# A two-layer decode step on one core: the fold's masks and sums on GpSimd, one row's LayerNorm on ScalarE and GpSimd, PV between the scores

## The chip, the cores and the metric

The kernel runs on one core of a Trainium2 chip. The metric is the device time of one execution in microseconds (us). The version before takes 1202.7 us, the median of three runs (1202.06 to 1204.01).

## The reference

Eight rows `x` (one token each, 512 numbers, bfloat16) go twice through the same two blocks, with the same weights and caches both times:

```
x = x + A(layernorm(x))     # attention: 32 query heads, 8 key/value heads,
                            # 8192 cached positions of 128 numbers, wq 512x4096, wo 4096x512
x = x + B(layernorm(x))     # silu(h @ w1) @ w2, w1 512x1792, w2 1792x512
```

A query head group of four shares one key/value head: scores are q.k / sqrt(128), softmax over the 8192 positions, then the sum of the values, then wo. Each row has its own cache of 8 x 8192 x 128 keys and as many values, in bfloat16: 128 MiB of keys and 128 MiB of values in all. In the second pass the caches are needed again.

## The kernel before, in words

**Tasks and positions.** A task is one (layer, row b, key/value head g): 2 x 8 x 8 = 128 tasks. Its keys and its values are 2 MiB each, loaded in four granules of 512 KB into slots of an arena (`NSLOT = 27` slots). A task has `GPT = 8` positions, two for each granule (`GPG = 2`). One Python loop over the position `p` writes all instructions in order; each engine then executes its own instructions in that order, with semaphores between engines.

**The order of the tasks.** Of a row's 32 key granules (8 heads of 4) the last `KEEP = 20`, heads 3 to 7, stay in the arena from layer 0 to layer 1. So a row's heads 3 to 7 in layer 0 ("kept" tasks) come shortly before the same heads in layer 1, which load values alone. Between them stand five or six tasks of heads 0 to 2 (of layer 0 of a later row, or of layer 1 of an earlier one), which load keys and values, four and four. Meanwhile the row's "chain" runs: output projection, residual, LayerNorm, MLP, LayerNorm and query projection of this one row, spread over the positions. `plan_loads` gives each load the position where it is needed and the one after which its slot is free; SyncE issues them in the order of need, and waits for the slot.

**One task, by lines of before.** VectorE transposes each key granule in place (L466), `LT` positions ahead of the position; TensorE makes the scores of the granule at the odd positions (L543). After the task, in the next eight positions (the table `soft`): `softmax_max` at 0 (VectorE L554, L556, then GpSimd's all-reduce over partitions `tops`, L559), `softmax_shift` and `softmax_exp` at 2 (VectorE L563, L566, ScalarE L570), `softmax_sum` at 4 (VectorE makes `ssm`, L577, GpSimd's all-reduce `ssa`, L580), `emit_pt` at 5 (TensorE transposes P, L589, ScalarE copies to PT, L593), `softmax_rcp` at 7 (L600). The values are multiplied `LP` positions after the scores (`emit_pv`, L608), at odd positions too, behind the scores.

**The fold.** The result of PV lies in a PSUM bank `OTp` as 128 partitions x 512: of each row only one of four blocks of 128 columns is its own. `emit_own` and `emit_fold` (`FOLD_AT` positions later) bring them together into 128 x 4. In most tasks ScalarE copies the bank to `E` (L624) and TensorE multiplies four blocks with masks `sel` (L640). In the tasks of layer 1 whose keys are kept (`eased`), VectorE masks and sums the four blocks (L629, L632) and TensorE does one multiplication with `hm` (L645). `emit_norm`, `FOLD` positions after the last PV's place, divides by the softmax sum (L655). `add_heads` multiplies four finished heads of a row with wo (L739).

**The chain.** `chain_of` is a list of stages. In each position as many are taken as are needed to end `EARLY = 4` positions ahead of the row's first task of layer 1. `ln_stages` has three: a sum and its all-reduce (L663, L665), centring, squares and their sum and all-reduce (L671 to L680), the reciprocal root by `NEWTON = 3` steps on VectorE (L685 to L699). `settle` adds `SETTLE` empty stages behind them; `project` cuts a projection into pieces (L721).

The initial all-reduces and the LayerNorm of all eight rows, at the start and at the end, go through the same functions with n = 8.

Of the kernel before, what the change touches and what calls it, by code (L numbers as in the profile page):

```python
# [5 lines left out]
HQ = 32  # L6
DH = 128
SM_SCALE = DH ** -0.5
LN_EPS = 1e-5
RSQRT_SEED = float(0x5F3759DF)  # L10
NEWTON = 3

GRP = 8
GPT = 8
GPG = 2
NSLOT = 27
KEEP = 20
LT = 2
PRE = 10
LP = 14  # L20
EARLY = 4
WO_FROM = 36
NTP = 2
# [7 lines left out]
PAIR = 2  # L31
REACH = 32767
PAIR_ALL = False
FOLD = 3
FOLD_AT = 2
ACT_FOLD = True
NQS = 4
CW = 32
SETTLE = 2

BF16 = mybir.dt.bfloat16
FP32 = mybir.dt.float32
# [181 lines left out]
def _build(ctx, nc, A_x, A_k_cache, A_v_cache, A_wq, A_wo, B_w1, B_w2, out):  # L224
# [68 lines left out]
    tr = sb([128, B], FP32, "tr")  # L293
    s1 = sb([128, B], FP32, "s1")
    s1a = sb([128, B], FP32, "s1a")
    xc = sb([128, KT, B], FP32, "xc")
    sq = sb([128, KT, B], FP32, "sq")
    xnT = sb([128, KT, B], BF16, "xnT")
# [88 lines left out]
    with nc.Block() as block:  # L387

        @block.sync
        def _(sync_eng):  # L390
# [183 lines left out]

            def softmax_sum(ti):
                st = ti % NST
                op(dve, lambda: dve.tensor_scalar(  # L577
                    ssm[st][:, :], hm[:, :], rs[st][:, 0:1], None, op0=ALU.mult),
                   reads=["hm", f"rs{st}"], writes=[f"ssm{st}"])
                op(pool, lambda: pool.partition_all_reduce(ssa[st][:, :], ssm[st][:, :], 128, bass.bass_isa.ReduceOp.add),  # L580
                   reads=[f"ssm{st}"], writes=[f"ssa{st}"])
# [32 lines left out]
                ]  # L614
                mm_group(steps, reads=[r_half(slot, 0), r_half(slot, 1), f"PT{pb}"], writes=[f"OT{ob}"])

            def eased(ti):
                layer, _b, g = tasks[ti]
                return layer == 1 and (g, 0) in kept

            def emit_own(ti):
                ob = ti % 2
                if not eased(ti) and ACT_FOLD:
                    op(act, lambda: act.copy(E[:, :], OTp[ob][:, :]), reads=[f"OT{ob}"], writes=["E"])  # L624
                    return
                for x in range(CPB):
                    ot = OTp[ob][:, x * DH:(x + 1) * DH]
                    if x == 0:
                        op(dve, lambda: dve.tensor_scalar(E[:, 0:DH], ot, own_x[:, 0:1], None, op0=ALU.mult),  # L629
                           reads=[f"OT{ob}", "own_x"], writes=["E"])  # L630
                    else:
                        op(dve, lambda x=x, ot=ot: dve.scalar_tensor_tensor(  # L632
                            E[:, 0:DH], ot, own_x[:, x:x + 1], E[:, 0:DH], op0=ALU.mult, op1=ALU.add),
                           reads=[f"OT{ob}", "own_x", "E"], writes=["E"])

            def emit_fold(ti):
                ob = ti % 2
                if not eased(ti) and ACT_FOLD:
                    steps = [
                        lambda x=x: pe.matmul(OTp[ob][:, 0:REP], E[:, x * DH:(x + 1) * DH], sel[:, x, :],  # L640
                                              start=(x == 0), stop=(x == CPB - 1))
                        for x in range(CPB)
                    ]
                else:
                    steps = [lambda: pe.matmul(OTp[ob][:, 0:REP], E[:, 0:DH], hm[:, :], start=True, stop=True)]  # L645
                mm_group(steps, reads=["E", "hm", "sel"], writes=[f"OT{ob}"])
# [11 lines left out]
            def ln_stages(xv, rx, n):  # L658

                xcv, sqv, xnv = xc[:, :, 0:n], sq[:, :, 0:n], xnT[:, :, 0:n]  # L660

                def first():
                    op(dve, lambda: dve.tensor_reduce(s1[:, 0:n], xv.rearrange("p k b -> p b k"), AX.X, ALU.add),  # L663
# [18 lines left out]
                def third():  # L682
                    v, y, t = vr[:, 0:n], yr[:, 0:n], tr[:, 0:n]
                    vi, yi = v.bitcast(INT32), y.bitcast(INT32)
                    op(dve, lambda: dve.tensor_scalar(v, s1a[:, 0:n], 1.0 / D, LN_EPS, op0=ALU.mult, op1=ALU.add),  # L685
                       reads=["s1a"], writes=["vr"])
                    op(dve, lambda: dve.tensor_scalar(yi, vi, 1, None, op0=ALU.logical_shift_right),
                       reads=["vr"], writes=["yr"])
                    op(dve, lambda: dve.tensor_scalar(yi, yi, -1.0, RSQRT_SEED, op0=ALU.mult, op1=ALU.add),
                       reads=["yr"], writes=["yr"])  # L690
                    if n == 1:
                        scale = 1.0
                        for _n in range(NEWTON):
                            op(dve, lambda: dve.tensor_scalar(t, y, y, v, op0=ALU.mult, op1=ALU.mult),  # L694
                               reads=["yr", "vr"], writes=["tr"])
                            op(dve, lambda: dve.tensor_scalar(y, t, -3.0 * scale ** 2, y, op0=ALU.add, op1=ALU.mult),  # L696
                               reads=["tr", "yr"], writes=["yr"])
                            scale *= -2.0 * scale ** 2
                        op(dve, lambda: dve.tensor_scalar(xnv, xcv, y, 1.0 / scale, op0=ALU.mult, op1=ALU.mult),  # L699
                           reads=["xc", "yr"], writes=["xnT"])  # L700
                        return
# [60 lines left out]
            def block_stages(xs, rxs, n, fine=False):  # L762

                x0, x1, x2 = xs
                r0, r1, r2 = rxs
                parts = 2 if fine else 1
# [12 lines left out]
                def attended():  # L779
                    add_residual(x1, r1, x0, r0, n, CW if n == 1 else n)  # L780

                st = [attended] + ln_stages(x1, r1, n) + settle
                st += joined(project(w1_sb, "w1", FT, KT, lambda k: xnT[:, k, 0:n], "xnT", n, parts), expo)
                st += [silu, idle]
                st += joined(
                    project(w2_sb, "w2", KT, FT, lambda k: hsT[:, k * n:(k + 1) * n], "hsT", n, parts),
                    lambda: add_residual(x2, r2, x1, r1, n, n))
                return st

            def joined(pieces, then):  # L790
                last = pieces[-1]
# [7 lines left out]
            def query(n, dst_of, rdst, parts=1):  # L799
                return joined(  # L800
                    project(wq_sb, "wq", HQ, KT, lambda k: xnT[:, k, 0:n], "xnT", n, parts),
                    lambda: op(
                        dve,
                        lambda: dve.tensor_copy(dst_of, MISC[:, 0:HQ * n].rearrange("p (h b) -> p h b", b=n)),
                        reads=["MISC"], writes=rdst,
                    ))

            def chain_of(b):
                xs = [XT[n][:, :, b:b + 1] for n in range(3)]
                st = block_stages(xs, ["XT0", "XT1", "XT2"], 1, True)  # L810
                st += ln_stages(xs[2], "XT2", 1) + settle
                return st + query(1, QT2[b % 2][:, 0:HQ].rearrange("p (h b) -> p h b", b=1), [f"QT2_{b % 2}"], 4)

            summed = [0] * (B + 1)
            heads = [[] for _ in range(B + 1)]
# [38 lines left out]
            first1 = {b: min(task_at[(1, b, g)] for g in range(HKV)) * GPT for b in range(B)}  # L854
            ntask = len(tasks)

            for p in range(NG + LP + GPT + FOLD + 1):
                tq = (p + LQ) // GPT
                if (p + LQ) % GPT == 0 and tq < ntask:
# [5 lines left out]
                emit_t_until(p + LT)  # L865
                if p % GPG == GPG - 1 and p < NG:
                    emit_s(p)
                if p % GPG == GPG - 1 and 0 <= p - LP < NG:
                    emit_pv(p - LP)
                copied = p - LP - GPT  # L870
                if copied >= 0 and copied % GPT == 0 and copied // GPT < ntask:
# [8 lines left out]
                if chain:  # L880
                    left = max(1, first1[chain_b[0]] - EARLY - p)
                    for _n in range(-(-len(chain) // left)):
                        chain.pop(0)()
                elif p >= WO_FROM and heads[turn[0]] and not (p < NG and tasks[p // GPT][0] and (tasks[p // GPT][2], 0) in kept
                                             and turn[0] < B):
                    add_heads(turn[0])
                done = p - LP - GPT - FOLD
                if done >= 0 and done % GPT == 0 and done // GPT < ntask:
# [61 lines left out]
```

## Time and profile before

| | |
|---|---|
| median of three runs | 1202.7 us (1202.06 to 1204.01) |
| the profiled execution | 1203.2 us, of which the span is 1201.2 us |
| TensorE busy | 811.5 us (68%), weight loads 505.4 us |
| VectorE busy | 735.7 us (61%) |
| ScalarE busy | 274.0 us (23%) |
| GpSimd busy | 117.9 us (10%), 300 instructions |
| DMA, loads | 465.12 MB, mean 389 GB/s, 99.2% of 16 engines' span |

Times are microseconds from the start of the span. The page's digits are the busy share of forty equal slices in tenths. In a timeline or a group, PE is TensorE, DVE VectorE, ACT ScalarE, POOL GpSimd, SP SyncE; a row of the timeline has the start, the duration, engine, line, operation and tiles, and in brackets the idle time of the engine before it and what ended that ("issue": nothing that the profile shows). In a row of windows the columns are the stretch, its length, the busy time of TensorE, its weight loads, VectorE, ScalarE and GpSimd with the number of instructions, the granted TensorE clock, DMA's share and GB/s. Reloads, waits and semaphores are not counted as busy.

### The profile page before, as it was taken

Reading aid. Unit: us, or ns where it says so; the run is one execution under the profiler, and the core shown is the slowest. Engines: PE = TensorE matmul, PEld = TensorE weight load, DVE = VectorE, ACT = ScalarE, POOL = GpSimd, SP = SyncE. Lnnn points to the kernel's source line nnn. Section 1 sums busy time; section 2 is a strip of 40 time slices with the busy share of each in tenths; the row PEclk is TensorE's granted clock in tenths of the full one; section 3 lists DMA queues with packets and bytes.
Section 4 is the critical chain, followed back from the end, with each engine's and each line's share of the span. In section 5 each row is a group of like instructions: output and inputs, shape, how many; then the busy total and the mean of one; then the engine's idle time right before and its main releaser. Section 6 shows DMA issues by size and latency. Waiting matters only on the chain.

```text
span 1201.2 us, 32533 instructions
## 1 busy us (share of the span) xinstructions
PE 811.5 (68%) x13960; PEld 505.4 (42%) x13960; DVE 735.7 (61%) x1858; ACT 274.0 (23%) x482; POOL 117.9 (10%) x300
## 2 busy tenths in 40 slices
PE   1537777576856686677757786667757676667865
PEld 1324444344524463345424454345434453345534
DVE  3736665767575655667476756657466756667472
ACT  0212123122312223221312132122312232121321
POOL 0000111001100111001100111001100111001100
PEclk9655576555855576555855566556755676555665
DMA  9999999999999999999999999999999999999993
GB/s 363 385 396 407 399 376 409 408 403 379 396 409 408 392 357 410 408 399 383 400 409 403 393 391 409 409 392 365 403 408 397 365 396 409 408 404 385 385 409 133
DMA packets 131568, 467.19 MB, mean 389 GB/s; under 512 B 13904, under 2 KB 19808, under 8 KB 130912
## 3 DMA queue, kind: packets, MB, share of 16 engines
q1 hardware_dynamic: 131424, 465.12, 99.2%
q8 instruction: 109, 1.79, 0.6%
q14 instruction: 35, 0.29, 0.1%
HBM read 465.05 MB, written 0.01 MB: 387 GB/s over the span
## 4 chain that ended last, share of the span: by engine, by line
DMA 59%; PE 15%; SPq 15%; DVE 7%; issue 3%; ACT 1%; POOL 1%; POOLq 0%; ACTq 0%; DVEq 0%
DMA arena<-in_A_v_cache_dram 48%; SPq L356 15%; DMA arena<-in_A_k_cache_dram 10%; PE OTp L608 5%; PE OTp L640 3%; PE MISC L721 3%; DVE arena L466 3%; PE SCp L543 3%; ACT P L570 1%; PE TPp L589 1%; DVE E L632 1%; DVE tr L694 1%; DVE yr L696 1%; DVE rowmax L554 0%; PE MISC L739 0%
## 5 line engine op out<-in xcount | busy, mean ns | idle before, releaser
L466 DVE STREAM_TRANSPOSE arena<-arena 128x1024 int32<-128x1024 int32 x352 | 436.0, 1240 | 239.1 <-DMA arena<-in_A_k_cache_dram 238.8
L608 PE MATMUL OTp<-arena,PT 128*16 128x512 bf16 x2048 | 283.0, 549 | 292.8 <-DMA arena<-in_A_v_cache_dram 289.9
L570 ACT ACTIVATE P<-SCp,shift 128x512 bf16<-128x512 f32 x128 | 180.4, 1409 | 646.2 <-PE SCp L543 234.1
L543 PE MATMUL SCp<-arena,QB 128*32 128x128 bf16 (+1 forms) x7040 | 275.6, 301 | 3.7 <-DVE mine L563 2.3
L608 PEld LDWEIGHTS OTp<-arena,PT 128*16 128x16 bf16 x2048 | 54.9, 97 | 383.6 <-DMA arena<-in_A_v_cache_dram 375.6
L543 PEld LDWEIGHTS SCp<-arena,QB 128*32 128x32 bf16 x7040 | 167.6, 122 | 63.8 <-issue 41.3
L640 PEld LDWEIGHTS OTp<-sel,E 128*128 128x128 f32 x704 | 140.3, 296 | 37.8 <-issue 25.6
L640 PE MATMUL OTp<-sel,E 128*128 128x4 f32 x704 | 147.9, 333 | 0.9 <-ACT E L624 0.7
L559 POOL PARTITION_ALL_REDUCE tops<-top x128 | 47.5, 371 | 563.1 <-DVE QT L655 241.6
L580 POOL PARTITION_ALL_REDUCE ssa<-ssm x128 | 55.2, 432 | 444.9 <-DVE ssm L577 423.4
L554 DVE TENSOR_REDUCE rowmax<-SCp 128x1 f32<-128x512 f32 x128 | 84.6, 661 | 21.4 <-PE SCp L543 20.9
L593 ACT COPY PT<-TPp 128x256 bf16<-128x256 bf16 x128 | 47.6, 372 | 211.7 <-PE TPp L589 211.7
L589 PE MATMUL TPp<-ident,P 128*128 128x128 bf16 x512 | 70.2, 283 | 12.4 <-ACT P L570 11.8
L589 PEld LDWEIGHTS TPp<-ident,P 128*128 128x128 bf16 x512 | 39.7, 121 | 66.2 <-issue 38.4
L577 DVE TENSOR_SCALAR ssm<-hm,rs 128x4 f32<-128x4 f32 x128 | 25.9, 202 | 66.5 <-ACT P L570 66.5
L624 ACT COPY E<-OTp 128x512 f32<-128x512 f32 x88 | 52.1, 592 | 4.1 <-PE OTp L608 4.1
L739 PEld LDWEIGHTS MISC<-at,wo 128*128 128x128 bf16 x1024 | 33.0, 105 | 34.2 <-DVE at L655 28.8
L721 PE MATMUL MISC<-xnT,wq 128*128 128x32 bf16 (+1 forms) x1152 | 35.5, 185 | 16.9 <-DVE xnT L708 15.7
L632 DVE SCALAR_TENSOR_TENSOR E<-OTp,own_x,E 128x128 f32<-128x128 f32 x120 | 42.1, 351 | 4.3
L721 PEld LDWEIGHTS MISC<-xnT,wq 128*128 128x128 bf16 x1152 | 34.4, 105 | 24.4 <-issue 22.1
L739 PE MATMUL MISC<-at,wo 128*128 128x32 bf16 x1024 | 38.2, 187 | 6.6 <-issue 1.3
L645 PE MATMUL OTp<-hm,E 128*128 128x4 f32 x80 | 20.5, 327 | 24.1 <-DVE E L632 24.1
(61 smaller groups left out, 359.3 us busy)
## 6 DMA issues: line engine op xcount, KB each, us to landing
arena<-in_A_v_cache_dram SPq DMA_DIRECT2D x512, 512.0 KB, 11.2
arena<-in_A_k_cache_dram SPq DMA_DIRECT2D x352, 512.0 KB, 14.9
wq<-in_A_wq_dram SPq DMA_DIRECT2D x1, 4096.0 KB, 16.4
wo<-in_A_wo_dram SPq DMA_DIRECT2D x1, 4096.0 KB, 26.0
w<-in_B_w_dram SPq DMA_DIRECT2D x2, 1792.0 KB, 22.6
P<-in_A_x_dram SPq DMA_DIRECT2D x1, 8.0 KB
out_dram<-P SPq DMA_DIRECT2D x1, 8.0 KB
```

The source lines that it names most:

```text
L356: eng.dma_start(out_ap, in_ap).then_inc(counter.sem, 16)
L466: op(dve, lambda: dve.transpose(words, words), reads=[r_half(slot, 0), r_half(slot, 1)], writes=[r_half(slot, 0), r_half(slot, 1)])
L543: lambda n=n, t=t, lo=lo, hi=hi, of=of: pe.matmul(SCp[bank][t * QUAD:(t + 1) * QUAD, lo * 128:hi * 128], QB[qn][:, n, :], of(t, n), start= ...
L554: op(dve, lambda: dve.tensor_reduce(rowmax[:, :], SCp[bank][:, :], AX.X, ALU.max), reads=[f"SC{bank}"], writes=["rowmax"])
L570: op(act, lambda: act.activation(P[:, :].rearrange("p (x j k) -> p k x j", x=CPB, k=NGRAN), SCp[bank][:, :].rearrange("p (k x j) -> p k x ...
L580: op(pool, lambda: pool.partition_all_reduce(ssa[st][:, :], ssm[st][:, :], 128, bass.bass_isa.ReduceOp.add), reads=[f"ssm{st}"], writes=[f ...
L589: lambda c=c: pe.transpose(tpv[:, c, :], P[:, c * 128:(c + 1) * 128], ident[:, :])
L608: lambda t=t: pe.matmul(OTp[ob][t * QUAD:t * QUAD + CPB * REP, :], PT[pb][:, k, t].rearrange("p x r -> p (x r)"), ARENA[:, slot * SLOT + t ...
L632: op(dve, lambda x=x, ot=ot: dve.scalar_tensor_tensor(E[:, 0:DH], ot, own_x[:, x:x + 1], E[:, 0:DH], op0=ALU.mult, op1=ALU.add), reads=[f" ...
L640: lambda x=x: pe.matmul(OTp[ob][:, 0:REP], E[:, x * DH:(x + 1) * DH], sel[:, x, :], start=(x == 0), stop=(x == CPB - 1))
L721: lambda o=o, k=k: pe.matmul(MISC[:, o * n:o * n + w], w_sb[:, k, o * 128:(o + 1) * 128], rhs_of(k).to_broadcast([128, w]) if n == 1 else ...
L739: lambda o=o, h=h: pe.matmul(MISC[:, o * w:(o + 1) * w], wo_sb[:, h, o * 128:(o + 1) * 128], rhs_of(h).to_broadcast([128, w]) if n == 1 el ...
```

## The change

- **Fold.** In every task but the last, ScalarE copies the bank to `E`; GpSimd multiplies it with the mask (512 columns) and adds halves twice (256 and 128 columns); TensorE does the one multiplication with `hm`. `FOLD_AT` goes from 2 to 4 positions, `FOLD` from 3 to 5.
- **LayerNorm of one row (n = 1).** The two sums are made by ScalarE (`accum_out`), centring, Newton steps and the last product by GpSimd; three VectorE steps remain. `SETTLE` goes from 2 to 4, and the residual's addition joins the first step (`along`).
- **softmax_sum** makes `ssm`, and the query its copy, on ScalarE instead of VectorE.
- **Places.** `LT` goes from 2 to 1 and `LP` from 14 to 13; PV stands at even positions, the scores at odd ones.
- **Output pieces.** `add_heads` of a row runs only from the row's kept tasks of layer 0 on (`calm`).

```diff
-LT = 2
+LT = 1
-LP = 14
+LP = 13
-FOLD = 3
-FOLD_AT = 2
-ACT_FOLD = True
+FOLD = 5
+FOLD_AT = 4
+PIECES = (2, 2, 4)
-SETTLE = 2
+SETTLE = 4
...
             def softmax_sum(ti):
-                op(dve, lambda: dve.tensor_scalar(
-                    ssm[st][:, :], hm[:, :], rs[st][:, 0:1], None, op0=ALU.mult),
+                op(act, lambda: act.activation(ssm[st][:, :], hm[:, :], ACT.Copy, scale=rs[st][:, 0:1]),
...
-            def eased(ti):
-                layer, _b, g = tasks[ti]
-                return layer == 1 and (g, 0) in kept
+            def straight(ti):
+                return ti == len(tasks) - 1
 
             def emit_own(ti):
                 ob = ti % 2
-                if not eased(ti) and ACT_FOLD:
-                    op(act, lambda: act.copy(E[:, :], OTp[ob][:, :]), reads=[f"OT{ob}"], writes=["E"])
+                op(act, lambda: act.copy(E[:, :], OTp[ob][:, :]), reads=[f"OT{ob}"], writes=["E"])
+                if straight(ti):
                     return
-                for x in range(CPB):
-                    ot = OTp[ob][:, x * DH:(x + 1) * DH]
...
+                ev = E[:, :].rearrange("p (x d) -> p x d", d=DH)
+                op(pool, lambda: pool.tensor_tensor(
+                    ev, ev, own_x[:, :].unsqueeze(2).to_broadcast([128, CPB, DH]), ALU.mult),
+                   reads=["E", "own_x"], writes=["E"])
+                n = CPB * DH // 2
+                while n >= DH:
+                    op(pool, lambda n=n: pool.tensor_tensor(E[:, 0:n], E[:, 0:n], E[:, n:2 * n], ALU.add),
+                       reads=["E"], writes=["E"])
+                    n //= 2
 
             def emit_fold(ti):
-                if not eased(ti) and ACT_FOLD:
+                if straight(ti):
...
+                def one_first():
+                    op(act, lambda: act.activation(sqv, xv, ACT.Copy, scale=-1.0 / D, accum_out=s1[:, 0:1]),
+                    op(pool, lambda: pool.partition_all_reduce(s1a[:, 0:1], s1[:, 0:1], 128, bass.bass_isa.ReduceOp.add),
+                def one_second():
+                    op(act, lambda: act.activation(sqv, xv, ACT.Square, bias=s1a[:, 0:1], accum_out=s2[:, 0:1]),
+                    op(pool, lambda: pool.tensor_scalar(
+                        xcv, xv, s1a[:, 0:1], -2.0 ** -13, op0=ALU.add, op1=ALU.mult),
+                    op(pool, lambda: pool.partition_all_reduce(s2a[:, 0:1], s2[:, 0:1], 128, bass.bass_isa.ReduceOp.add),
+                def one_third():
...
+                    for _n in range(NEWTON):
+                        op(pool, lambda: pool.tensor_scalar(t, y, y, v, op0=ALU.mult, op1=ALU.mult),
+                        op(pool, lambda scale=scale: pool.tensor_scalar(
+                            y, t, -3.0 * scale ** 2, y, op0=ALU.add, op1=ALU.mult),
+                        scale *= -2.0 * scale ** 2
+                    op(pool, lambda: pool.tensor_scalar(xnv, xcv, y, None, op0=ALU.mult),
+                if n == 1:
+                    return [one_first, one_second, one_third]
...
+            def along(stages, more):
+                return stages[:-1] + joined(stages[-1:], more[0]) + more[1:]
...
+            def calm(p):
+                if p >= NG:
+                    return False
+                return p >= task_at[(0, turn[0], kept_from)] * GPT
...
-                if p % GPG == GPG - 1 and 0 <= p - LP < NG:
+                if (p - LP) % GPG == GPG - 1 and 0 <= p - LP < NG:
                     emit_pv(p - LP)
...
-                elif p >= WO_FROM and heads[turn[0]] and not (p < NG and tasks[p // GPT][0] and (tasks[p // GPT][2], 0) in kept
-                                             and turn[0] < B):
+                elif p >= WO_FROM and heads[turn[0]] and (turn[0] == B or calm(p)):
                     add_heads(turn[0])
```

More of the change, by code (lines that the diff above doesn't have):

```diff
@@ L295, in _build @@
     s1a = sb([128, B], FP32, "s1a")
+    s2 = sb([128, 1], FP32, "s2")
+    s2a = sb([128, 1], FP32, "s2a")
     xc = sb([128, KT, B], FP32, "xc")
@@ L615, in emit_pv @@
                 mm_group(steps, reads=[r_half(slot, 0), r_half(slot, 1), f"PT{pb}"], writes=[f"OT{ob}"])
-            def eased(ti):
-                layer, _b, g = tasks[ti]
-                return layer == 1 and (g, 0) in kept
+            def straight(ti):
+                return ti == len(tasks) - 1
             def emit_own(ti):
                 ob = ti % 2
-                if not eased(ti) and ACT_FOLD:
-                    op(act, lambda: act.copy(E[:, :], OTp[ob][:, :]), reads=[f"OT{ob}"], writes=["E"])
+                op(act, lambda: act.copy(E[:, :], OTp[ob][:, :]), reads=[f"OT{ob}"], writes=["E"])
+                if straight(ti):
                     return
-                for x in range(CPB):
-                    ot = OTp[ob][:, x * DH:(x + 1) * DH]
[L628 to L634, printed above, removed]
+                ev = E[:, :].rearrange("p (x d) -> p x d", d=DH)
[7 more added lines that the diff above has]
+                    n //= 2
             def emit_fold(ti):
                 ob = ti % 2
-                if not eased(ti) and ACT_FOLD:
+                if straight(ti):
                     steps = [
@@ L660, in ln_stages @@
                 xcv, sqv, xnv = xc[:, :, 0:n], sq[:, :, 0:n], xnT[:, :, 0:n]
+                def one_first():
+                    op(act, lambda: act.activation(sqv, xv, ACT.Copy, scale=-1.0 / D, accum_out=s1[:, 0:1]),
+                       reads=[rx], writes=["sq", "s1"])
+                    op(pool, lambda: pool.partition_all_reduce(s1a[:, 0:1], s1[:, 0:1], 128, bass.bass_isa.ReduceOp.add),
+                       reads=["s1"], writes=["s1a"])
+                def one_second():
+                    op(act, lambda: act.activation(sqv, xv, ACT.Square, bias=s1a[:, 0:1], accum_out=s2[:, 0:1]),
+                       reads=[rx, "s1a"], writes=["sq", "s2"])
+                    op(pool, lambda: pool.tensor_scalar(
+                        xcv, xv, s1a[:, 0:1], -2.0 ** -13, op0=ALU.add, op1=ALU.mult),
+                       reads=[rx, "s1a"], writes=["xc"])
+                    op(pool, lambda: pool.partition_all_reduce(s2a[:, 0:1], s2[:, 0:1], 128, bass.bass_isa.ReduceOp.add),
+                       reads=["s2"], writes=["s2a"])
@@ new lines, in one_third @@
+                def one_third():
+                    v, y, t = vr[:, 0:1], yr[:, 0:1], tr[:, 0:1]
+                    vi, yi = v.bitcast(INT32), y.bitcast(INT32)
+                    op(dve, lambda: dve.tensor_scalar(v, s2a[:, 0:1], 1.0 / D, LN_EPS, op0=ALU.mult, op1=ALU.add),
+                       reads=["s2a"], writes=["vr"])
+                    op(dve, lambda: dve.tensor_scalar(yi, vi, 1, None, op0=ALU.logical_shift_right),
+                       reads=["vr"], writes=["yr"])
+                    op(dve, lambda: dve.tensor_scalar(yi, yi, -1.0, RSQRT_SEED, op0=ALU.mult, op1=ALU.add),
+                       reads=["yr"], writes=["yr"])
+                    scale = 1.0
+                    for _n in range(NEWTON):
+                        op(pool, lambda: pool.tensor_scalar(t, y, y, v, op0=ALU.mult, op1=ALU.mult),
+                           reads=["yr", "vr"], writes=["tr"])
+                        op(pool, lambda scale=scale: pool.tensor_scalar(
+                            y, t, -3.0 * scale ** 2, y, op0=ALU.add, op1=ALU.mult),
+                           reads=["tr", "yr"], writes=["yr"])
+                        scale *= -2.0 * scale ** 2
+                    assert scale == -2.0 ** 13
+                    op(pool, lambda: pool.tensor_scalar(xnv, xcv, y, None, op0=ALU.mult),
+                       reads=["xc", "yr"], writes=["xnT"])
@@ L690, in third @@
                        reads=["yr"], writes=["yr"])
[L691 to L701, printed above, removed]
                     for _n in range(NEWTON):
@@ L765, in block_stages @@
                 r0, r1, r2 = rxs
-                parts = 2 if fine else 1
+                p1, p2 = PIECES[:2] if fine else (1, 1)
                 def expo():
@@ L780, in attended @@
                     add_residual(x1, r1, x0, r0, n, CW if n == 1 else n)
-                st = [attended] + ln_stages(x1, r1, n) + settle
-                st += joined(project(w1_sb, "w1", FT, KT, lambda k: xnT[:, k, 0:n], "xnT", n, parts), expo)
+                st = along([attended], ln_stages(x1, r1, n)) + settle
+                st += joined(project(w1_sb, "w1", FT, KT, lambda k: xnT[:, k, 0:n], "xnT", n, p1), expo)
                 st += [silu, idle]
-                st += joined(
-                    project(w2_sb, "w2", KT, FT, lambda k: hsT[:, k * n:(k + 1) * n], "hsT", n, parts),
+                return st + joined(
+                    project(w2_sb, "w2", KT, FT, lambda k: hsT[:, k * n:(k + 1) * n], "hsT", n, p2),
                     lambda: add_residual(x2, r2, x1, r1, n, n))
-                return st
+            def along(stages, more):
+                return stages[:-1] + joined(stages[-1:], more[0]) + more[1:]
             def joined(pieces, then):
@@ L802, in query @@
                     lambda: op(
-                        dve,
-                        lambda: dve.tensor_copy(dst_of, MISC[:, 0:HQ * n].rearrange("p (h b) -> p h b", b=n)),
+                        *((act, lambda: act.copy(dst_of, MISC[:, 0:HQ * n].rearrange("p (h b) -> p h b", b=n)))
+                          if n == 1 else
+                          (dve, lambda: dve.tensor_copy(dst_of, MISC[:, 0:HQ * n].rearrange("p (h b) -> p h b", b=n)))),
                         reads=["MISC"], writes=rdst,
@@ L810, in chain_of @@
                 st = block_stages(xs, ["XT0", "XT1", "XT2"], 1, True)
-                st += ln_stages(xs[2], "XT2", 1) + settle
-                return st + query(1, QT2[b % 2][:, 0:HQ].rearrange("p (h b) -> p h b", b=1), [f"QT2_{b % 2}"], 4)
+                st = along(st, ln_stages(xs[2], "XT2", 1)) + settle
+                return st + query(1, QT2[b % 2][:, 0:HQ].rearrange("p (h b) -> p h b", b=1), [f"QT2_{b % 2}"], PIECES[2])
             summed = [0] * (B + 1)
@@ L855, in _ @@
             ntask = len(tasks)
+            kept_from = min(g for g, _k in kept)
+            def calm(p):
+                if p >= NG:
+                    return False
+                return p >= task_at[(0, turn[0], kept_from)] * GPT
             for p in range(NG + LP + GPT + FOLD + 1):
```

## The prediction

> **What bounds the kernel now.** I read the page's slices and queue line first, then windows of 10 us, and last GpSimd's own timeline.
>
> ```profile
> DMA  9999999999999999999999999999999999999993
> GB/s 363 385 396 407 399 376 409 408 403 379 396 409 408 392 357 410 408 399 383 400 409 403 393 391 409 409 392 365 403 408 397 365 396 409 408 404 385 385 409 133
> ...
> q1 hardware_dynamic: 131424, 465.12, 99.2%
> ```
> ```profile
> 230.00:240.00 10.00, 7.05 (x112) 4.26 (x105) 6.35 (x12) 2.04 (x5) 0.80 (x2) 0.50 1.02 408
> 430.00:440.00 10.00, 7.86 (x183) 6.34 (x183) 6.70 (x16) 1.42 (x2) 0.37 (x1) 0.66 1.00 362
> 1190.00:1200.00 10.00, 3.90 (x116) 3.44 (x116) 4.42 (x18) 0.26 (x1) 0.00 (x0) 0.50 0.00 0
> ```
> The loads bound it: 465.12 MB at the best rate seen, 408 GB/s, take 1140 us of the 1201.2. The other 61 us are a start that lags by about 6, a tail of 18.5 after the last load lands (1182.7), and some 36 in dips such as 430:440, where an item's MLP chain runs. A task outside the kept ones of layer 1 loads eight times 512 KB, so DMA's pace is 8 x 524,288 B / 409 GB/s = 10.25 us a task, 1.28 us a position. GpSimd is almost idle: 0.80 us in 10.
>
> That idleness is where the change puts its work, so the last view is GpSimd's timeline, with VectorE's row that made its input:
>
> ```profile
> 9.18 0.28 POOL L396 TENSOR_SCALAR_AFFINE_SELECT ident<-ident 128x128 bf16<-128x128 bf16 x1 [8.19 <-issue]
> 9.43 0.34 POOL L403 MEMSET QB<- 128x128 bf16 x2
> 21.10 0.43 POOL L665 PARTITION_ALL_REDUCE s1a<-s  x1 [11.33 <-issue]
> 22.32 0.40 POOL L680 PARTITION_ALL_REDUCE s1a<-s  x1 [0.79 <-DVE s L678]
> ...
> 11.52 0.21 DVE L663 TENSOR_REDUCE s<-XT 128x8 f32<-128x32 bf16 x1
> ```
> The affine select reads nothing but what GpSimd wrote itself at 0.79, yet starts at 9.18. The first all-reduce had its input at 11.73 (11.52 + 0.21) and GpSimd free at 9.77, yet starts at 21.10; the second follows at once. In both gaps ("issue") no instruction is shown. The instruction list of the built program names them: directly ahead of the affine select stands a reload of GpSimd's library of routines with index 0, directly ahead of that all-reduce one with index 1; memset needs none. So going from one kind of operation to the other cost 8.19 and 11.33 us. From there on all 292 GpSimd instructions are all-reduces, and no third reload is needed.
>
> **The change, part by part.** The decisive part is in no line of the diff. Masks and sums of the fold (tensor_tensor) and the Newton steps (tensor_scalar) need library 0, the softmax all-reduces library 1, and one GpSimd queue holds them in turn: tops, ssa, reload 0, multiply, add, add, reload 1, tops, and so on. The list of the changed program has 304 reloads (152 of each) against 2: about 250 for the 127 folds, the rest around 16 LayerNorms. So 302 are added.
>
> What else one task needs of GpSimd comes from these rows:
>
> ```profile
> 449.32 0.37 POOL L559 PARTITION_ALL_REDUCE tops<-top  x1 [1.32 <-DVE top L556]
> ...
> 450.21 1.39 ACT L570 ACTIVATE P<-SCp,shift 128x512 bf16<-128x512 f32 x1 [1.65 <-PE OTp L608]
> ...
> 451.96 0.43 POOL L580 PARTITION_ALL_REDUCE ssa<-ssm  x1 [2.27 <-DVE ssm L577]
> ```
> tops 0.37, then 2.27 in which ssa waits for shift, exponential and ssm, then ssa 0.43. No tensor_tensor of GpSimd is in the trace. Its 512 + 256 + 128 columns are seven blocks of 128; bounds are 0.17 us a block (the memset above, 0.34 for two) and twice VectorE's 0.351 (L632), so 1.2 to 4.9; I take VectorE's 0.351 a block, the nearest that does arithmetic, 2.46 us. [...]
>
> Each step waits for the one before: the next task's tops stands behind the fold in the queue, and VectorE's shift, the exponential, the transposes of P and, in TensorE's order, all later scores and PVs stand behind tops. So nothing hides a reload but the short E copy. Per task: 0.37 + 2.27 + 0.43 + 2.46 = 5.53 us and two reloads. Against the pace of 10.25 us, GpSimd takes over as bound once a reload costs more than (10.25 - 5.53) / 2 = 2.36 us.
>
> A reload's price: 8.19 was measured while DMA moved 279 GB/s (first 10 us), 11.33 at about 406. If GpSimd bounds, traffic is far less (467 MB in 3.3 ms is 141 GB/s), so 8.19 is the nearer row and I take it. A straight line through the two, closed on itself, gives 5.77 at 181 GB/s; if instead the difference belongs to the libraries, the mean is 9.76. [...]
>
> The sum: 38 until the first exponential (37.7), 128 x 5.53 = 708, 16 LayerNorms at 4.3 = 69 (two all-reduces 0.4 each, eight small GpSimd steps at VectorE's 0.25, two ScalarE steps at 0.45, three VectorE steps at 0.2), a tail of 17 after the last loads' PV (1184.4 to 1201.2): 832. Reloads 302 x 8.19 = 2473. Span 3305; with the 2.0 around it (1203.2 against 1201.2; the median 1202.7 lies 0.5 lower) 3307.
>
> The other parts are hidden under that. For the rival below they are: **Fold**: TensorE spends 147.9 / 88 = 1.68 us a fold (L640), with one matmul 20.5 / 40 = 0.51 (L645): 1.17 less in 88 tasks; VectorE loses 40 x (0.32 + 3 x 0.351) = 55 us of masks (L629, L632), ScalarE gains 40 copies of 0.59. **LayerNorm**: about 2.4 us a time leave VectorE (L663 to L678, L694 to L699), where key transposes stood behind them. **ssm and query copies** on ScalarE: some 0.2 us each, ScalarE being busy 2.04 in 10; no cost. **LT and PV's place**: a key slot waits two positions between transposition and score, not three, 1.28 us earlier free; but PV now directly follows the transposes of P and waits for the PT copy behind the E copy (0.37 + 0.59), about 1 us a task, covered by TensorE's 2.95 idle in 10 at 230:240 and 128 us if that were gone. **Output pieces**: 64 groups of 0.6 us (L739) move to the kept loads, under the same idle time. **Stages**: four waits instead of two twice, attended joined to the first LayerNorm step; an item's chain has 23 entries instead of 21, in one position less.
>
> **The rivals.** *Faster: a reload costs nothing after the first of each library.* Then GpSimd needs 5.53 of 10.25 us a task, the parts above act, and about half of the 36 us in the dips comes back: 1203.2 - 18 = 1185. [...] Against: the list repeats the reload every time, with the index of the other library. It decides below 2.36 us a reload. *Every reload costs 11.33*, since loads run whenever slots come free: 832 + 3422 + 2 = 4256. Against: loads would be in flight a third of the time. [...] *Reloads hide, but GpSimd's small steps cost 1 us each instead of 0.25*: the seven on the way to xnT hold TensorE 5.3 us longer per LayerNorm, less 2.6 for two loads of lead, so 16 x 2.7 = 43 over 1185: 1228.
>
> **How the numbers follow.** Forecast, reloads between 5.77 and 9.76: 0.80, span by these 2578 to 3782. 11.33: 0.04. Near 4: 0.04. Free reloads: 0.08. Slow small steps: 0.03. The parts cancel: 0.01. The range 2560 to 3800 leaves out 0.20. Faster by over 0.2% (about what a measurement can tell here) 0.08, within it 0.01, slower 0.80 + 0.04 + 0.04 + 0.03 = 0.91.
>
> **What would show it.** Right: GpSimd's idle time before tops (now L561) and before the fold's multiply (L627) is some 8 us each, over 120 times, ended by "issue"; exponentials of neighbouring tasks lie about 22 us apart; GB/s near 140; TensorE and ScalarE wait for E and tops. Partly wrong: the same pattern with gaps under 5.8 or over 9.8. Wrong: GB/s stays near 400, tops starts within a microsecond of top, and tasks stay 10.25 us apart.

## The result, and the profile after

The changed kernel takes 2856.9 us (2845.9 to 2861.3), the kernel before 1202.4 beside it: ratio 2.37, with a 95% interval of [2.366, 2.383]. The profiled execution took 2852.8 us, its span is 2851.1. The forecast was 3307, its range 2560 to 3800.

The page of after, first the lines that answer to those of before:

```profile
PE 757.0 (27%) x13710; PEld 454.4 (16%) x13710; DVE 625.0 (22%) x1386; ACT 332.8 (12%) x722; POOL 439.1 (15%) x809
...
DMA  9653553436444463435634265443635355343550
GB/s 375 261 191 119 185 199 125 156 119 221 163 141 142 137 226 124 170 111 177 207 105 176 92 223 173 140 156 123 231 126 178 116 177 203 121 175 126 188 181 1
...
q1 hardware_dynamic: 131424, 465.12, 47.7%
...
issue 69%; POOL 13%; PE 6%; DVE 6%; ACT 5%; DMA 1%; POOLq 0%; ACTq 0%; DVEq 0%
```

The same 465.12 MB are loaded, but the loads are spread over 2851 us, and no engine is busy for more than 27% of it. The last line is the chain that ended last: 69% of the span went by while an engine waited for nothing that the profile shows. A reader who looks for the bound among busy times finds none. It is in the idle times of GpSimd's groups (busy, mean ns | idle before them and what ended it):

```profile
L627 POOL TENSOR_TENSOR E<-E,own_x 128x512 f32<-128x512 f32 x127 | 130.8, 1030 | 920.8 <-issue 920.8
L581 POOL PARTITION_ALL_REDUCE ssa<-ssm x128 | 56.5, 441 | 316.0 <-ACT ssm L579 263.9 <-issue 47.5 <-ACT eh L797 4.6
L561 POOL PARTITION_ALL_REDUCE tops<-top x128 | 49.4, 386 | 772.5 <-issue 758.0 <-DVE top L558 14.5
L688 POOL TENSOR_SCALAR tr<-yr,vr 128x1 f32<-128x1 f32 x48 | 16.2, 338 | 117.3 <-issue 114.0
...
L674 POOL PARTITION_ALL_REDUCE s2a<-s x16 | 6.4, 401 | 96.4 <-issue 96.4
...
L671 POOL TENSOR_SCALAR xc<-XT,s1a 128x4 f32<-128x4 bf16 x16 | 4.2, 264 | 112.1 <-issue 111.9
```

Each group that stands first behind a change of library has an idle time ended by "issue": ahead of the fold's multiply (L627), of the next task's tops (L561), and at three or four places of each LayerNorm. These six and the two at the start (8.2 and 10.1) make 2066.9 us, 72% of the span. The list of waits says how many there are, and who waits for them:

```profile
DVE mine L565 <- POOL tops L561: 1575.1, 126, 17.1
...
PE OTp L645 <- POOL E L632: 949.2, 119, 14.4
POOL E L627 <- issue: 920.8, 121, 12.2
POOL tops L561 <- issue: 758.0, 126, 8.4
```

VectorE's step for the softmax shift waits 1575 us for tops, TensorE's fold 949 us for E: both stand right behind a gap. The trace does name the reload, in rows of GpSimd's sequencer, which count as no busy time (the view of one source line: number, shortest/median/longest ns, first and last start):

```profile
L627 POOLq MODIFY_POOL_CONFIG  x242: 82/85/85, 44.5 to 2822.5; - x121
```
```profile
L561 POOLq MODIFY_POOL_CONFIG  x252: 11/11/11, 54.6 to 2813.6; - x126
```

Two such rows of 85 or 11 ns stand ahead of each gap, twice 121 and twice 126, as many as the gaps in the waits; over all lines there are 608, two for each of the 304 reloads of the built program. The instruction is short, what follows it is not. The trace of before has such rows too, at 1.0 us ahead of the affine select and at 10.0 us ahead of the first all-reduce, so its two gaps are not as nameless as the prediction read them:

```profile
L396 POOLq MODIFY_POOL_CONFIG  x2: 11/11/11, 1.0 to 1.0; - x2
```
```profile
L665 POOLq MODIFY_POOL_CONFIG  x2: 1/1/1, 10.0 to 10.0; - x2
```

One task in the timeline of after, GpSimd alone, and behind it the row of VectorE that made the second tops' input:

```profile
1306.48 0.44 POOL L581 PARTITION_ALL_REDUCE ssa<-ssm  x1 [2.31 <-ACT ssm L579]
1314.74 1.03 POOL L627 TENSOR_TENSOR E<-E,own_x 128x512 f32<-128x512 f32 x1 [7.81 <-issue]
1315.84 1.26 POOL L632 TENSOR_TENSOR E<-E 128x256 f32<-128x256 f32 x2
1322.93 0.39 POOL L561 PARTITION_ALL_REDUCE tops<-top  x1 [5.83 <-issue]
...
1309.74 0.22 DVE L558 SCALAR_TENSOR_TENSOR top<-hm,rowmax,far 128x4 f32<-128x4 f32 x1
```

`top` was ready at 1309.96; tops started 12.97 us later, because it stands behind the fold in GpSimd's queue and behind the second reload. Exponentials are 19.42 us apart here (1304.66 and 1324.08 in the same timeline), of which 13.64 are the two gaps.

### The profile page after: what moved, and what is told of

The parts are those of the page before. It is cut to its first block, busy times and chain, and to the rows that moved or that the text cites. A ratio compares the mean times of both kernels' runs of the same rounds, so it can differ in the third digit from the quotient of the medians.

```text
span 2851.1 us, 33075 instructions
## 1 busy us (share of the span) xinstructions
PE 757.0 (27%) x13710; PEld 454.4 (16%) x13710; DVE 625.0 (22%) x1386; ACT 332.8 (12%) x722; POOL 439.1 (15%) x809
## 2 busy tenths in 40 slices
DMA packets 131574, 467.22 MB, mean 164 GB/s; under 512 B 13904, under 2 KB 19808, under 8 KB 130912
## 3 DMA queue, kind: packets, MB, share of 16 engines
q1 hardware_dynamic: 131424, 465.12, 47.7%
## 4 chain that ended last, share of the span: by engine, by line
issue 69%; POOL 13%; PE 6%; DVE 6%; ACT 5%; DMA 1%; POOLq 0%; ACTq 0%; DVEq 0%
POOL E L632 5%; POOL E L627 4%; ACT P L572 3%; DVE arena L468 3%; POOL tops L561 2%; PE SCp L545 2%; ACT PT L594 1%; PE TPp L590 1%; PE MISC L749 1%; PE OTp L609 1%; ACT E L623 1%; PE MISC L767 1%; DVE mine L565 1%; DVE shift L568 1%; POOL tr L688 1%
## 5 line engine op out<-in xcount | busy, mean ns | idle before, releaser
L545 PE MATMUL SCp<-arena,QB 128*32 128x128 bf16 (+1 forms) x7312 | 307.3, 319 | 428.0 <-DVE arena L468 386.7
L565 DVE SCALAR_TENSOR_TENSOR mine<-tops,hm 128x4 f32<-128x4 f32 x128 | 20.8, 162 | 1575.1 <-POOL tops L561 1575.1
L609 PE MATMUL OTp<-arena,PT 128*16 128x512 bf16 x2048 | 313.6, 601 | 74.5 <-ACT PT L594 52.0
L645 PE MATMUL OTp<-hm,E 128*128 128x4 f32 x254 | 74.7, 364 | 949.2 <-POOL E L632 949.2
L545 PEld LDWEIGHTS SCp<-arena,QB 128*32 128x32 bf16 x7312 | 210.5, 134 | 556.6 <-DVE arena L468 427.7
L627 POOL TENSOR_TENSOR E<-E,own_x 128x512 f32<-128x512 f32 x127 | 130.8, 1030 | 920.8 <-issue 920.8
L645 PEld LDWEIGHTS OTp<-hm,E 128*128 128x128 f32 x254 | 63.5, 311 | 998.8 <-POOL E L632 997.2
L561 POOL PARTITION_ALL_REDUCE tops<-top x128 | 49.4, 386 | 772.5 <-issue 758.0
L632 POOL TENSOR_TENSOR E<-E 128x256 f32<-128x256 f32 x254 | 149.6, 589 | 19.9
L623 ACT COPY E<-OTp 128x512 f32<-128x512 f32 x128 | 72.4, 566 | 11.6 <-PE OTp L609 11.5
L601 DVE RECIPROCAL rcp<-ssa 128x4 f32<-128x4 f32 x128 | 19.7, 154 | 185.5 <-POOL ssa L581 185.2
```

The source lines that it names most:

```text
L545: lambda n=n, t=t, lo=lo, hi=hi, of=of: pe.matmul(SCp[bank][t * QUAD:(t + 1) * QUAD, lo * 128:hi * 128], QB[qn][:, n, :], of(t, n), start= ...
L561: op(pool, lambda: pool.partition_all_reduce(tops[:, :], top[:, :], 128, bass.bass_isa.ReduceOp.max), reads=["top"], writes=["tops"])
L609: lambda t=t: pe.matmul(OTp[ob][t * QUAD:t * QUAD + CPB * REP, :], PT[pb][:, k, t].rearrange("p x r -> p (x r)"), ARENA[:, slot * SLOT + t ...
L627: op(pool, lambda: pool.tensor_tensor(ev, ev, own_x[:, :].unsqueeze(2).to_broadcast([128, CPB, DH]), ALU.mult), reads=["E", "own_x"], writ ...
L632: op(pool, lambda n=n: pool.tensor_tensor(E[:, 0:n], E[:, 0:n], E[:, n:2 * n], ALU.add), reads=["E"], writes=["E"])
```

## The experiments

The theory is the prediction's: the time is the reloads, one for each change between library 0 (multiply, add, tensor_scalar) and library 1 (all-reduce over partitions), whatever the instructions between them cost. The rivals: GpSimd's arithmetic or the new places of the steps make the loss; or the reloads are dear only in this order of work.

**1. No arithmetic on GpSimd.** After, with the fold as before (ScalarE's copy and four products, VectorE in the eased tasks) and the LayerNorm's tensor_scalar steps on VectorE. Its program has 2 reloads.

```diff
-                    op(pool, lambda: pool.tensor_scalar(
+                    op(dve, lambda: dve.tensor_scalar(
                         xcv, xv, s1a[:, 0:1], -2.0 ** -13, op0=ALU.add, op1=ALU.mult),
...
             def emit_own(ti):
-                op(act, lambda: act.copy(E[:, :], OTp[ob][:, :]), reads=[f"OT{ob}"], writes=["E"])
-                if straight(ti):
+                if not eased(ti) and ACT_FOLD:
+                    op(act, lambda: act.copy(E[:, :], OTp[ob][:, :]), reads=[f"OT{ob}"], writes=["E"])
                     return
```

> The changed kernel with its GpSimd arithmetic taken back: the fold is made as before (ScalarE copy and four products with sel, VectorE in the eased tasks), and the one-row LayerNorm's centring, Newton steps and last product run on VectorE. LT, LP, PV's place, FOLD, FOLD_AT, SETTLE, the output pieces and ssm on ScalarE stay as changed. The program has 2 reloads, as before. Theory (the 302 reloads are the whole loss): near 1200 or below, 1185 to 1203, tasks 10.25 us apart. Rival (PV directly behind the transposes of P, or the later fold, holds up the queues): over 1300 even without a reload.

Measured: 1209.6 us, ratio 1.0063 [1.0043, 1.0082]. 1647 of the 1654 us are gone. What is left of the change with the old fold is a loss of 7 us, above the 1185 to 1203 us that were expected; runs 6 to 12 are on that.

**2. The arithmetic stays, the reloads go.** After, with the all-reduces of tasks and chain replaced by a tensor_scalar of the same tile, so that GpSimd needs library 0 alone (4 reloads in all). The maxima and sums over partitions are left out in it.

```diff
-                op(pool, lambda: pool.partition_all_reduce(tops[:, :], top[:, :], 128, bass.bass_isa.ReduceOp.max),
+                op(pool, lambda: pool.tensor_scalar(tops[:, :], top[:, :], 1.0, None, op0=ALU.mult),
...
-                op(pool, lambda: pool.partition_all_reduce(ssa[st][:, :], ssm[st][:, :], 128, bass.bass_isa.ReduceOp.add),
+                op(pool, lambda: pool.tensor_scalar(ssa[st][:, :], ssm[st][:, :], 1.0, None, op0=ALU.add),
```

> The changed kernel with all GpSimd arithmetic kept, but without library 1 in the tasks and the chain: each all-reduce over partitions there is replaced by a tensor_scalar of the same tile, so the sums and maxima are each partition's own and the output is not the reference's. The program has 4 reloads. Theory (reloads): 1175 to 1200, as the loads bound it again; about 1185 by the first rival's sum. Rival (GpSimd's fold of 2.3 us and its place in the queue make the loss): stays far over 1300, because every fold instruction stands where it stood.

Measured: 1183.5 us, ratio 0.9847 [0.9828, 0.9866]. From its page:

```profile
PE 716.2 (61%) x13710; PEld 431.0 (36%) x13710; DVE 640.8 (54%) x1386; ACT 341.9 (29%) x722; POOL 386.2 (33%) x809
...
L627 POOL TENSOR_TENSOR E<-E,own_x 128x512 f32<-128x512 f32 x127 | 132.0, 1039 | 108.0 <-ACT E L623 108.0
```

The same 809 GpSimd instructions, the same multiply at 1.04 us, but it now waits for its input (ScalarE's E), 108 us in all, and no longer for "issue". With 386 us busy GpSimd is far from a bound. So the arithmetic isn't the loss.

**3 and 8. Reloads alone, put into the kernel before.** One addition of a 128x1 tile on GpSimd, in each task (254 reloads more) or in each fourth (64 more), and nothing else of the change:

```diff
+                op(pool, lambda: pool.tensor_tensor(tick[:, :], tick[:, :], tick[:, :], ALU.add), reads=["tick"], writes=["tick"])
```

> The kernel before with one GpSimd tensor_tensor of 128x1 added in each task, at the place of the fold's copy, that nothing waits for. 256 reloads, 254 more than before; nothing else is changed. Theory (reloads): 7.6 + 6.0 for the two reloads as in the changed kernel's gaps, plus tops 0.37, 2.27 and ssa 0.43 make 16.7 us a task, so 128 x 16.7 = 2140 and about 55 at the ends: 2150 to 2250. Rival (the fold's arithmetic or the moved places): within 10 us of 1203.

> The kernel before with the 128x1 tensor_tensor in every fourth task: 64 reloads more, a quarter of those of the touch in each task. Theory: a pair of reloads holds the softmax for some 19 us once in 41 us of loads; in the kept tasks twelve issued loads (15 us) cover most of it, in the others about five (6 us) do. 32 pairs lose 5 to 12 us each: 1360 to 1590, and not a quarter of the way (1515) by rule. Rival (a loss that is proportional and nothing hidden): 1515 or more.

Measured, in one execution each: 2454.1 us in each task, 1458.3 in each fourth. Groups of the first, then of the second:

```profile
L561 POOL PARTITION_ALL_REDUCE tops<-top x128 | 49.7, 388 | 986.4 <-issue 964.7 <-DVE top L558 15.2 <-DVE arena L468 6.5
L625 POOL TENSOR_TENSOR tick<-tick 128x1 f32<-128x1 f32 x128 | 23.6, 185 | 970.8 <-issue 970.8
```
```profile
L561 POOL PARTITION_ALL_REDUCE tops<-top x128 | 48.0, 375 | 601.8 <-issue 257.9 <-DVE QT L659 153.3 <-DVE top L558 104.0
...
L626 POOL TENSOR_TENSOR tick<-tick 128x1 f32<-128x1 f32 x32 | 5.8, 183 | 302.9 <-issue 302.9
```

128 additions with 23.6 us of work in all double the time of the kernel before. The first run lies above what was expected (2150 to 2250): tops' gap is 964.7 / 123 = 7.84 us there, not the 6.0 that was taken over from after. With fewer reloads the loads run faster (319 GB/s over the span, against 190 in each task) and each gap is longer: 302.9 / 32 = 9.47 and 257.9 / 32 = 8.06. Still 64 reloads cost 255 us, 4.0 each, and 254 cost 1252, 4.9 each, while the gaps last 8.76 and 7.74 us on average: part of a gap is hidden, more of it where the gaps are rare. The loss isn't proportional (a quarter of 1252 would give 1515 us). That the loads issued ahead hide it, as was expected, was not tested by itself.

**4 and 5. The two halves of the change.** After with the LayerNorm's arithmetic back on VectorE (fold alone on GpSimd, 254 reloads more), and after with the fold back (LayerNorm alone, 64 more).

```diff
-                        op(pool, lambda: pool.tensor_scalar(t, y, y, v, op0=ALU.mult, op1=ALU.mult),
+                        op(dve, lambda: dve.tensor_scalar(t, y, y, v, op0=ALU.mult, op1=ALU.mult),
```

> The changed kernel with the one-row LayerNorm's arithmetic on VectorE instead of GpSimd; the fold stays on GpSimd. 256 reloads instead of 304. Theory (reloads): the tasks stay 18.8 us apart, 128 x 18.8 = 2406 and about 55 at the ends, a few us for each LayerNorm: 2450 to 2520. Rival (the LayerNorm on GpSimd is the larger part): under 2000.

> The changed kernel with the fold as before and only the one-row LayerNorm's arithmetic on GpSimd. 66 reloads instead of 304, about four for each of the 16 LayerNorms. Theory (reloads at 6.0 to 7.6 us): each LayerNorm holds GpSimd about 27 us, in which the tasks' softmax and so everything else stops, less about 7 of lead of the loads: 1210 + 16 x 20 = 1530, 1400 to 1650. Rival (the LayerNorm's steps on GpSimd are cheap and hidden): 1200 to 1220.

Measured, in one execution each: 2517.0 and 1571.3 us, as expected. Against run 1 the fold costs 1307 us, the LayerNorm 362; together 1669, against 1647 for both. The LayerNorm's 64 reloads cost 5.65 us each, more than the 4.0 of run 8, although their gaps are shorter (465.6 / 64 = 7.28 us): less of them is hidden. Likely that is because four of them follow each other in one LayerNorm; no run shows it apart.

**6 and 7. The rest of the change without reloads.** Run 1 left 7 us to explain. These two use another cheap fold, with no GpSimd in it: `E` and the masks `sel` in bfloat16, in all tasks ScalarE's copy and four products. Run 6 is run 1 with that fold, run 7 the kernel before with it.

```diff
-    E = sb([128, CPB * DH], FP32, "E")
+    E = sb([128, CPB * DH], BF16, "E")
...
-    sel = sb([128, CPB, REP], FP32, "sel")
+    sel = sb([128, CPB, REP], BF16, "sel")
```

> The version without GpSimd arithmetic (fold and LayerNorm taken back) with E and sel in bfloat16, so that the fold's four products on TensorE are one pass each; all tasks the same way. 2 reloads. Theory (what the change could give is TensorE's 1.2 us a fold, which the one-library version got and the version with the old fold did not): 1180 to 1195. Rival (the gain of the one-library version came from the LayerNorm off VectorE or from the missing all-reduces): stays at 1205 to 1212.

> The kernel before with nothing changed but E and sel in bfloat16 and the fold the same way in all tasks. Theory: the fold's 1.7 us on TensorE leave the dips; 1183 to 1197. Rival (the dips come from the chain's own waits): 1198 to 1205.

Measured: 1188.7 us, ratio 0.9881 [0.9853, 0.991], and 1196.6, ratio 0.9953 [0.9931, 0.9974]. Run 6 beats both kernels. The four products of a fold keep TensorE busy for 34.1 / 128 = 0.27 us there, in run 1 for 151.8 / 88 = 1.73, where each product in 32-bit floats is two rows of the trace (704 for 88 folds) and in bfloat16 one (512 for 128):

```profile
L626 PE MATMUL OTp<-sel,E 128*128 128x4 bf16 x512 | 34.1, 171 | 0.8 <-ACT E L621 0.7
```
```profile
L642 PE MATMUL OTp<-sel,E 128*128 128x4 f32 x704 | 151.8, 339 | 0.7 <-ACT E L626 0.7
```

**9 and 10. Two suspects.** Run 9 is run 6 with `SETTLE` back at 2; run 10 has besides the output pieces at their old places.

```diff
-SETTLE = 4
+SETTLE = 2
...
-                elif p >= WO_FROM and heads[turn[0]] and (turn[0] == B or calm(p)):
+                elif p >= WO_FROM and heads[turn[0]] and not (p < NG and tasks[p // GPT][0] and (tasks[p // GPT][2], 0) in kept
+                                             and turn[0] < B):
```

> The version with the rest of the change and the bfloat16 fold, with SETTLE = 2 as before instead of 4: 19 stages for an item's chain instead of 23 in the same 18 positions, so hardly any position takes two. In the version with 4, one task of each item took 13.3 to 15.1 us instead of 10.25. Theory (that stall comes from stages taken two at a time): about 2 us back for each of seven items, 1172 to 1184. Rival (it comes from TensorE waiting for the LayerNorm, and fewer empty stages lengthen that): 1189 to 1200.

> The same with the output pieces placed as before (not held back to the kept loads). Theory (pieces of 0.6 us hide under TensorE's idle time in both places): within 3 us of the version with SETTLE = 2 alone. Rival (they add to the dips that the chain makes): 4 to 10 us slower than it.

Measured: 1188.6, ratio 0.9889 [0.9869, 0.9908], and 1187.6, ratio 0.9879 [0.9855, 0.9904]. Neither the empty stages nor the pieces' places make a difference; that the empty stages cost run 6 several us was wrong.

**11 and 12. PV back behind the scores.** Run 1 (32-bit fold) and run 6 (bfloat16 fold) with the old places:

```diff
-LT = 1
+LT = 2
...
-LP = 13
+LP = 14
```

> e1 (fold as before, LayerNorm steps on VectorE, no GpSimd arithmetic) with LT = 2 and LP = 14, so that PV stands at odd positions behind the scores again, as before the change. Theory: the 7 us that e1 lost against before come from PV's new place, where it waits for the copies of P's transposes behind four products in 32-bit floats: then 1200 to 1205. Rival: they come from the chain's and the fold's new due times (FOLD_AT 4, SETTLE 4, pieces): then it stays at 1207 to 1213.

> e6 (the same with a bfloat16 fold in all tasks, 1188.7) with LT = 2 and LP = 14. Theory: with the short fold PV's new place and the later transposition of keys are a gain, since key slots come free one position earlier: going back costs 5 to 9 us, 1194 to 1197, near e7's 1196.6. Rival: the place is worth nothing and the gain over e7 is the LayerNorm's two sums, ssm and the query copy on ScalarE: then it stays at 1186 to 1191.

Measured: 1212.8, ratio 1.0091 [1.0061, 1.0122], and 1201.0, ratio 0.9995 [0.9977, 1.0014]. So PV's new place and the later transposition are a gain with the short fold: 1.1%, 12 us, more than expected. With the old fold the intervals of runs 1 and 11 overlap; 0.3% is not clear of the noise. The theory that they cost run 1 its 7 us fell. What the runs leave: with PV at its old place and the same fold, the remaining edits (the fold's later due times, the LayerNorm's sums, ssm and the query copy on ScalarE) lose 0.9% with the old fold (run 11 against before) and 0.4% with the short one (run 12 against run 7). Which of them it is was not separated.

## Why the prediction was right

**What bounds after.** Right: reloads that the diff doesn't show, in one GpSimd queue with the softmax's two all-reduces. Run 2 keeps the work without the reloads and is faster than before; run 3 has reloads without the work and is twice as slow. The 303 gaps that end with "issue" stand against 304 reloads in the built program; the last one ends when VectorE's input comes.

**The price of a reload.** This term was mis-sized, and makes nearly the whole difference. 8.19 us were taken from the affine select's gap, for both libraries; the mean is 2066.9 / 303 = 6.82. The 301 after the first two took 2048.6 us, where 302 x 8.19 = 2473 had been put: 424 of the 454 us between the predicted and the measured span. The step that failed was to take the nearer of two rows as it stood: that row was measured at 279 GB/s, after runs at 164, and it is a row of index 0 alone. The straight line through the two rows, which gave the lower end 5.77 at 181 GB/s, had the direction right and went too far. The two rows differed in library and in traffic at once, and could not be told apart. In after they differ the other way round: 151 gaps ahead of library 0 take 1146.7 us, 7.59 each, and 150 ahead of library 1 901.9, 6.01 each. So 8.19 was 0.6 too high for index 0 and 2.2 too high for index 1, and of the 424 us index 1 makes 327. In run 3 the means are alike (7.64 and 7.84), but not the gaps behind the last load:

```profile
2417.18 0.18 POOL L625 TENSOR_TENSOR tick<-tick 128x1 f32<-128x1 f32 x1 [6.78 <-issue]
2423.39 0.39 POOL L561 PARTITION_ALL_REDUCE tops<-top  x1 [6.03 <-issue]
```

In after the shortest gap of index 0 is 6.64 us, of index 1 5.66; in its two halves the means differ the same way, 7.76 and 5.96 in run 4, 8.57 and 5.98 in run 5. So in after the least that a reload takes goes with the index, and when in the stream of loads it falls can add to that; the last section looks at how much.

Where loads are light, index 1 took 5.83 us at 154 GB/s; index 0 took 6.87 with no load at all (last section). The mean is 6.82, and each return to the other library pays it anew: 303 gaps for 304 reloads.

**The rest of the sum.** 832 us were predicted; 2851.1 - 2066.9 + the 18.3 of the first two gaps = 802.5 were measured. The fold took 1.03 + 0.07 + 1.26 = 2.36 us (2.46 predicted from VectorE's row), tops 0.386, ssa 0.441, the wait for ssm 2.31 us in the task shown and 2.59 in the next (2.27 predicted). The small LayerNorm steps took 0.26 to 0.34 us, not 0.25, and the 1 us of a rival not at all. The 30 us that are left are not assigned to a step.

**The signs.** Exponentials 19.42 us apart instead of 22, 164 GB/s instead of 140, gaps of 7.6 and 6.0 instead of 8: all from the price. The point of 2.36 us a reload, above which GpSimd would take over, is the prediction's estimate and was not tried: the shortest gap in after is 5.66 us. The 4 us a reload that the prediction gave 0.04 is no gap of after either; as a net loss run 8 had 4.0 us a reload, with gaps of 8.76 on average.

**The rival with free reloads.** 1185 us were predicted for it; run 2, where almost none are left, took 1183.5. Its parts cannot be read off as they were put: PV's new place was costed at nothing and gains 12 us beside the short fold (run 12 against run 6), and the remaining edits lose 5 to 11. So it is in part luck that the sum came within 2 us. Run 2 also has a cheaper step than an all-reduce (0.226 against 0.386 and 0.441 us), so it is not the changed kernel without reloads to the last microsecond.

## What to carry to other kernels

An idle engine is not a free one: before work is moved to GpSimd, look which library of routines each of its operations needs, and count in the built program how often the queue goes from one to the other; here a 128x1 addition a task took the kernel from 1202.6 to 2454.1 us. Where a profile shows no busy engine and a chain of "issue", look at the idle time ahead of the groups of one engine, and at its sequencer's rows (here MODIFY_POOL_CONFIG, already in the trace of before). A price seen only once or twice in a trace is sized with what ran beside it, and its range is kept wide.

## What the runs showed that was not expected

**A reload is not in the DMA records.** The queues of after, beside those of before, show the loads' bytes alone: 302 reloads add no queue and no megabyte (467.22 MB in all queues, against 467.19).

```profile
q8 instruction: 107, 1.75, 0.3%
q14 instruction: 43, 0.35, 0.0%
```

Before had 109 and 35 packets. The price isn't the same everywhere in the loads. Windows in after, each one whole gap: index 0 and index 1 behind the last load, index 0 and index 1 at the full rate of the loads, the gap of index 0 from the task shown, and the longest of all, which is index 0 too; behind it the longest cut in four:

```profile
2785.51:2792.38 6.87, 1.91 (x41) 1.14 (x40) 3.32 (x6) 0.37 (x1) 0.01 (x2) 0.50 0.00 0
2794.74:2800.81 6.07, 1.55 (x22) 0.99 (x22) 0.00 (x0) 0.00 (x0) 0.00 (x1) 0.50 0.00 0
82.72:90.28 7.56, 2.37 (x57) 1.51 (x55) 3.36 (x6) 0.37 (x1) 0.01 (x2) 0.50 1.03 410
92.64:99.07 6.43, 1.55 (x22) 0.99 (x22) 0.00 (x0) 0.00 (x0) 0.00 (x0) 0.50 1.02 406
1306.92:1314.74 7.82, 1.92 (x28) 0.83 (x26) 1.91 (x4) 0.37 (x1) 0.01 (x2) 0.50 0.70 258
1175.70:1187.94 12.24, 1.90 (x41) 1.14 (x40) 3.31 (x6) 0.37 (x1) 0.00 (x1) 0.50 0.70 257
```
```profile
1175.70:1178.70 3.00, 1.90 (x41) 1.14 (x40) 2.56 (x6) 0.37 (x1) 0.00 (x0) 0.50 0.94 345
1178.70:1181.70 3.00, 0.00 (x0) 0.00 (x0) 0.75 (x1) 0.00 (x0) 0.00 (x0) 0.50 0.88 289
1181.70:1184.70 3.00, 0.00 (x0) 0.00 (x0) 0.00 (x0) 0.00 (x0) 0.00 (x0) 0.50 0.94 373
1184.70:1187.94 3.24, 0.00 (x0) 0.00 (x0) 0.00 (x0) 0.00 (x0) 0.00 (x1) 0.50 0.09 37
```

Without any load a reload takes 6.87 and 6.07 us here, and the DMA records show no traffic in that time. In the longest gap two loads had been issued ahead and four more followed in its first 2.7 us; the reload ended some 3 us after the traffic had stopped. That looks like a reload that waits until the loads have drained. But at 410 and 406 GB/s, with no pause in the traffic, a reload took only 0.7 and 0.4 us more than without loads, and two gaps with the same mean traffic (257 and 258 GB/s) last 12.24 and 7.82 us. So neither the traffic nor the wait for a drain sets the price by itself. What makes some gaps of index 0 last 10 to 12 us stays open.

**Edits of a few microseconds don't add up.** The same PV place is worth 12 us beside a short fold; beside a long one no gain is clear of the noise.
